# One 512 KB piece of V per batch is sent to the lower 64 partitions of two slots

## The chip, the core and the metric

The kernel runs on one core of a Trainium2 chip. The time is that of one execution on the device in microseconds (us). The core has five engines that take part here: PE (TensorE: matrix products and transposes into PSUM), DVE (VectorE), ACT (ScalarE), POOL (GpSimd), and SP (SyncE), which in this kernel issues every data transfer. Transfers are carried out by 16 DMA engines. A tile in SBUF has 128 partitions. Each transfer raises its semaphore by 16 when its data has landed.

## The reference

Two layers are applied one after the other to x of shape [8, 1, 448] (8 batches, one query position, 448 channels). Each layer is an attention block and an MLP block, with residual sums:

```
x = x + A(layernorm(x))      # attention against the caches
x = x + B(layernorm(x))      # small MLP with a shift mixer
x = x + A(layernorm(x))      # the same caches and weights again
x = x + B(layernorm(x))

A: q = (x @ wq) as 16 heads of 256; k, v: caches [8 batches, 8 kv heads, 4096 keys, 256], two query heads per kv head
   p = softmax(q k^T / 16);  o = p v;  result = o @ wo
```

All arrays are bf16. The caches are by far the largest: K and V of one kv head are 4096 x 256 values, 2 MB each, so each cache is 128 MB. Every key of a head counts alike, so the keys may be taken in any order, as long as K and V have the same one.

## The kernel before, in words

**Tiles.** A slab in SBUF is cut into 31 slots (`NSLOT`), each 128 partitions x 2048 bf16, that is 512 KB. A head's K or V (2 MB) is loaded as four pieces c = 0 to 3 of one slot each. Partition p of the four pieces holds the keys 32p to 32p+31, piece c the keys 8c to 8c+7 of these, so a piece is 128 rows of 4096 B in memory. `chunks` (L444) makes these pieces and says with `most` how many neighbouring pieces may go in one transfer (1, 2 or 4 slots in a row, with rows of 4, 8 or 16 KB).

**Stages.** The work is cut by layer, batch b (0 to 7), and pair m (0 to 3) of two kv heads s = 0, 1. For each of them `kpart` (L836) builds the transposes of K, the scores, the softmax; `vpart` (L1034) the product with V. In `kpart` most K pieces are transposed by DVE in 32 x 32 blocks (`square`, L911 to L914), a few by PE with an ACT copy (L889 to L893); the scores are matrix products with K as the fixed operand (L919 to L925). The probabilities are exponentiated into `pT` (L1006), transposed by PE and DVE (L1013, L1021). The few pieces whose K went through PE have their probabilities in other places, copied by POOL (L1010) or ACT (L1027); a buffer `pN` of its own (there are two, `NZ`) serves this in layer 0 for m = 2 and 3. `vpart` then takes four matrix products per piece of V (`pv`, L1081 to L1091): 8 columns of probabilities as the fixed operand, 512 columns of V as the moving one.

**Order.** Layer 0 of batch b, the small MLP between (`turn(b)`), layer 1 of batch b and layer 0 of batch b+1 are woven together by the lists at L1216 to L1245. K pieces of layer 0 for m = 1, 2, 3 stay in their slots for layer 1; K of m = 0 is loaded again there, and V is always loaded anew. K(1, b, 0) comes together with V(1, b, 1); V(1, b, 0) comes with the first K of batch b+1.

**Queues.** `Plan.schedule` (L168) is a planner that runs over all operations with a cost for each, gives every engine one fixed order, and gives every transfer its slot. A transfer waits on SP for the readers of its slot's former content, in the order of `order` (L1248), and the transfers behind it wait with it. All transfers go out on one queue that feeds all 16 DMA engines. On its engine an operation waits in order, by semaphores.

Of the kernel before, what the change touches and what calls it, by code (L numbers as in the profile page):

```python
# [3 lines left out]
P = 128  # L4
B = 8
# [6 lines left out]
NCH = 4  # L12
NSLOT = 31
SMALL = 218
SLOT = 2048
# [5 lines left out]
NN = ((1, 0, 1, 1), (0, 0, 1, 1))  # L21
NZ = 2
WIDE = ((1, 0),)
MOST = (4, 4, 4, 2)
DRY4 = 4000.0
STILL = (False, False)
# [46 lines left out]
class Unit:  # L73


    def __init__(self, name, emit, nbytes, slotted=True):
        self.name, self.emit, self.nbytes, self.slotted = name, emit, nbytes, slotted
        self.wide = None
        self.slot = self.sem = self.val = None
        self.op = None  # L80
        self.readers = []
        self.land = None
        self.evs = [None, None]
        self.raw, self.source = False, None
        self.group, self.lead, self.pair = [self], None, None


class Plan:
# [9 lines left out]
    def add(self, eng, emit, cost, reads=(), writes=(), banks=(), units=(), prio=None, name="", n=4):  # L98
        o = Op(eng, emit, cost, self.prio if prio is None else prio, self.turn, name)
        o.n = n  # L100
        for b in reads:
            for w in b.writers:
                o.deps[w] = True
            b.readers.append(o)
        for b in writes:
            for w in b.writers:
                o.deps.setdefault(w, w.eng == eng and eng != "pe")
            for r in b.readers:
                if r is not o:
                    o.deps.setdefault(r, False)  # L110
            if o in b.readers:
                b.readers = [o]
            else:
                b.readers = []
            b.writers = [o]
        for k in banks:
            if k.eng == eng:
                for d in k.before:
                    o.deps.setdefault(d, False)
                k.ops.append(o)  # L120
            else:
                for d in k.ops:
                    o.deps.setdefault(d, False)
                k.before, k.ops, k.eng = k.ops, [o], eng
        for u in units:
            if u.op is not None:
                o.deps[u.op] = True
            u.readers.append(o)
        o.deps.pop(o, None)
        self.ops.append(o)  # L130
        return o
# [227 lines left out]
def bass_interleave_layers__gqa_block_cached__mixer_s_mlp__decode_kernel(  # L359
# [25 lines left out]
    slab = sb("slots", [P, SLOT * NSLOT], bf)  # L385
    slots = [slab[:, SLOT * i:SLOT * i + SLOT] for i in range(NSLOT)]
# [6 lines left out]
    ident = sb("ident", [P, P], bf)  # L393
# [3 lines left out]
    pT = [sb(f"pT{i}", [P, 192], bf) for i in range(NP)]  # L397

    pN = [sb(f"pN{i}", [P, 48], bf) for i in range(NZ)]
# [17 lines left out]
    psS = [nc.alloc_psum_tensor(f"psS{i}", [P, 512], f32) for i in range(NS)]  # L417
    psV = [nc.alloc_psum_tensor(f"psV{i}", [P, 512], f32) for i in range(NV)]
# [3 lines left out]
    bS = [Bank() for _ in range(NS)]  # L422
    bV = [Bank() for _ in range(NV)]
    bT, bX = Bank(), Bank()

    plan = Plan()
    add = plan.add
# [13 lines left out]
    U_wo = [rows(f"wo{i}", wo_sb[:, 8 * i:8 * i + 8, :], wo_src[:, 8 * i:8 * i + 8, :], P * 7168 * 1.1) for i in range(4)]  # L441
    U_w4 = [rows("w4", w4_sb[:, :, :], B_w4.rearrange("(t m) n -> m t n", m=P), P * 12544 * 1.1)]

    def chunks(cache, b, h, name, skip=(), most=2):  # L444


        src = cache[b, h].rearrange("(p j) d -> p (j d)", p=P)

        def emit(e, u):
            c, n = int(u.name[-1]), len(u.group)  # L450
            return e.dma_start(slab[:, SLOT * u.slot:SLOT * (u.slot + n)], src[:, SLOT * c:SLOT * (c + n)])
        us = [None if c in skip else Unit(f"{name}{c}", emit, P * 4096) for c in range(NCH)]
        for i in range(0, NCH, most):
            group = [u for u in us[i:i + most] if u is not None]
            if len(group) == most:
                plan.load(group[0], mates=group[1:])
            else:
                for u in group:
                    plan.load(u)
        return us  # L460


    Bc = Buf()
# [41 lines left out]
    BpT, BpZ, Brc = ([Buf() for _ in range(NP)] for _ in range(3))  # L505
    BpN = [Buf() for _ in range(NZ)]
# [302 lines left out]
    free_p, free_n = list(range(NP)), list(range(NZ))  # L809
# [4 lines left out]
    def apart(t):  # L814

        return t.rearrange("p (a c u r) -> p a c r u", a=4, u=3, r=4)[:, :, :, :, 0:3:2]
# [19 lines left out]
    def kpart(at, layer, b, m, kept, most=2):  # L836
# [12 lines left out]
        nS[0] += 1  # L849
        p.x = x  # L850
        p.y = y = free_p.pop(0)
        p.z = z = free_n.pop(0) if layer == 0 and m > 1 else None
        plan.prio = at
        p.K, p.kload = [], []
        for s in range(2):
            us = chunks(A_k_cache, b, 2 * m + s, f"{n}K{s}", [c for c in range(NCH) if (s, c) in kept], most)
            for c in range(NCH):
                if (s, c) in kept:
                    p.K.append(kept[s, c])
                    continue  # L860
                u = us[c]
                if u.lead is None:
                    p.kload.append(u)
                if c >= nns[s]:
                    v = Unit(f"{n}J{s}{c}", None, 0)
                    v.source, u.raw = u, True
                    if c % 2 and c - 1 >= nns[s]:
                        v.pair, p.K[-1].pair = p.K[-1], v
                    p.K.append(v)
                else:  # L870
                    p.K.append(u)
# [153 lines left out]
        for c in range(nn if z is None else 0):  # L1025
            ss = slice(sum(c >= w for w in nns), 2)
            add("act", lambda e, c=c, ss=ss: e.activation(apart(pT[y])[:, :, c, :, ss], xs.rearrange("p (a c r s) -> p a c r s", a=4, c=4, r=4)[:, :, c, :, ss],  # L1027
                                                          ACT.Exp, scale=INV_SQRT_DH), 230, [], [BpT[y]], [bS[x]], prio=pr, name=n + f"pn{c}")
        add("pool", lambda g: g.partition_all_reduce(db, rs, P, ReduceOp.add), 450, [B_["pm"]], [B_["gm"]], prio=pr + 1, name=n + "db")
        R = add("dve", lambda e: e.reciprocal(rc, db), 70, [B_["gm"]], [Brc[y]], prio=pr + 1, name=n + "rc")  # L1030
        R.deps = {d: data or d.eng == "dve" for d, data in R.deps.items()}
# [2 lines left out]
    def vpart(at, p, still, bank, most, aside):  # L1034
# [2 lines left out]
        own_ = lambda s, c: z is not None and c < p.nns[s]  # L1037
        Bp = lambda s, c: [BpN[z]] if own_(s, c) else [BpT[y], BpZ[y]]
        plan.prio = at
        p.V = [u for s in range(2) for u in chunks(A_v_cache, b, 2 * m + s, f"{n}V{s}", (), most)]  # L1040
        p.vload = [u for u in p.V if u.lead is None]
        if layer == 0:
            out_, bo = o1[b % 2][:, 8 * m:8 * m + 8], Bo1[b % 2][m]
        else:
# [3 lines left out]
        if still:  # L1048
            x = bank
            for s in range(2):  # L1050
                for c in range(NCH):
                    u = p.V[NCH * s + c]

                    def pv(e, u=u, c=c, s=s):
                        for cc in range(2):
                            o = psV[x][:, 16 * s + 4 * c + 2 * cc:16 * s + 4 * c + 2 * cc + 2]
                            for j in range(8):
                                i = j * DH + cc * P
                                if c < p.nns[s]:
                                    w = apart(pN[z] if own_(s, c) else pT[y])[:, j // 2, c, 2 * (j % 2):2 * (j % 2) + 2, s]  # L1060
                                else:
                                    w = apart(pT[y])[:, j % 4, p.place(s, c), 2 * (j // 4):2 * (j // 4) + 2, s]
                                last = e.matmul(o, slots[u.slot][:, i:i + P], w, start=(j == 0), stop=(j == 7))  # L1063
                        return last
# [8 lines left out]
        else:  # L1073
# [3 lines left out]
            for s in range(2):  # L1077
                for c in range(NCH):
                    u = p.V[NCH * s + c]

                    def pv(e, u=u, c=c, s=s):  # L1081
                        for i in range(4):
                            o = 12 * (NCH * i + p.place(s, c)) + 4 * s
                            w = pN[z][:, 12 * i + 4 * s:12 * i + 4 * s + 8] if own_(s, c) else pT[y][:, o:o + 8]
                            if c < p.nns[s]:
                                v = slots[u.slot][:, 512 * i:512 * i + 512].rearrange("p (k d) -> p k d", k=2)
                            else:
                                v = slots[u.slot].rearrange("p (k j d) -> p j k d", k=2, j=4)[:, i]
                            last = e.matmul(psV[x][32 * i:32 * i + 8, :].rearrange("p (k d) -> p k d", k=2), w, v,  # L1089
                                            start=(s == 0 and c == 0), stop=(s == 1 and c == NCH - 1))  # L1090
                        return last  # L1091
                    o = add("pe", pv, 430, Bp(s, c), [], [bV[x]], [u], prio=at + 0.02 * (NCH * s + c), name=f"{n}V{s}{c}", n=4)
                    if s or c:
                        o.deps[first] = True
                    else:
                        first = o
# [24 lines left out]
                for d in Bq1[b].readers + Bq1[b].writers:  # L1121
                    O.deps.setdefault(d, False)
        free_p.append(y)
        if z is not None:
            free_n.append(z)

    Bst = [{k: Buf() for k in ("pm", "gm", "mx")} for _ in range(NS)]
    red, Bred = sf[:, 0:8], [Bs[k] for k in ("sq", "f", "f1")]
# [263 lines left out]
```

## Time and profile before

| what | value |
|---|---|
| median of 3 runs | 1098.31 us (1097.34 to 1099.51) |
| the profiled execution's own time | 1098.74 us |
| its span (first to last instruction) | 1095.7 us |
| DVE busy | 832.6 us, 76% of the span |
| PE busy (matrix products) | 756.3 us, 69% |
| ACT busy, POOL busy | 207.8 us, 71.4 us |
| data moved by DMA | 448.94 MB, mean 410 GB/s |
| time in packets of the data queue q1 | 98.4% of 16 engines over the span |

How to read it: shares are of the span. The busy time of the DMA engines is the time that their packets took, summed over the 16 engines, so 100% means that all 16 had a packet under way all the time. Queue q1 carries the data that SP's transfers ask for, q8 and q14 carry instructions of the program itself. The times of the profiled execution and of the runs differ by 0.43 us at the median; 0.2% of the time is 2.2 us.

### The profile page before, as it was taken

How to read it: one execution, taken by the hardware profiler on the slowest of the kernel's cores; microseconds unless marked ns; L12 is line 12 of the kernel's file. 1: busy time of each engine (PE TensorE's matmuls, PEld its weight loads, DVE VectorE, ACT ScalarE, POOL GpSimd, SP SyncE). 2: the span in 40 equal slices, each digit the busy share in tenths (PEclk: the TensorE clock that was granted, in tenths of full speed). 3: DMA queues.
4: the chain of work that ended last, by engine and by line, in shares of the span. 5: the costliest groups of instructions: out<-in, count | busy, mean ns of one | idle time of the engine just before them, and what ended most of it. 6: DMA issues, size and time to landing. Idle time of an engine off the chain costs nothing.

```text
span 1095.7 us, 33703 instructions
## 1 busy us (share of the span) xinstructions
PE 756.3 (69%) x15400; PEld 526.6 (48%) x15400; DVE 832.6 (76%) x1595; ACT 207.8 (19%) x314; POOL 71.4 (7%) x232
## 2 busy tenths in 40 slices
PE   2566586778577865867767787577666786676864
PEld 2355454465346543555436554355444654356533
DVE  4999459964997499955899469984799739995572
ACT  1032121112021211203112032121221121121210
POOL 0000000000000000000000000000100000000000
PEclk9997566556655665556655556555655566555665
DMA  9999999999999999999999999999999999999994
GB/s 353 406 419 420 395 406 426 422 412 408 429 423 415 412 425 427 421 405 409 424 426 420 411 412 429 426 417 394 427 427 423 419 399 428 427 422 411 410 427 176
DMA packets 54846, 448.94 MB, mean 410 GB/s; under 512 B 5536, under 2 KB 11568, under 8 KB 14128
## 3 DMA queue, kind: packets, MB, share of 16 engines
q1 hardware_dynamic: 54704, 446.80, 98.4%
q8 instruction: 120, 1.97, 0.7%
q14 instruction: 22, 0.18, 0.0%
HBM read 446.77 MB, written 0.01 MB: 408 GB/s over the span
## 4 chain that ended last, share of the span: by engine, by line
DVE 39%; DMA 24%; PE 21%; issue 9%; ACT 3%; POOL 0%; POOLq 0%; DVEq 0%
DVE slots L914 29%; DMA slots<-in_A_k_cache_dram 16%; DMA slots<-in_A_v_cache_dram 8%; PE psV L1089 6%; PE psS L923 5%; DVE pT L1021 2%; PE psT L678 2%; ACT slots L892 2%; PE psS L902 2%; DVE slots L1102 1%; PE psV L1063 1%; PE psT L607 1%; PE psK L832 1%; PE psT L1138 1%; DVE qe L643 1%
## 5 line engine op out<-in xcount | busy, mean ns | idle before, releaser
L914 DVE STREAM_TRANSPOSE slots<-slots 128x1024 bf16<-128x1024 bf16 x544 | 649.4, 1228 | 33.0 <-DMA slots<-in_A_k_cache_dram 24.3
L923 PE MATMUL psS<-qe,slots 128*128 128x8 bf16 x5760 | 225.3, 175 | 152.6 <-DVE slots L914 111.5
L923 PEld LDWEIGHTS psS<-qe,slots 128*128 128x128 bf16 x5760 | 191.1, 104 | 238.5 <-DVE slots L914 176.0
L1089 PE MATMUL psV<-slots,pT 128*8 128x512 bf16 x1528 | 181.1, 550 | 17.5 <-DMA slots<-in_A_v_cache_dram 9.5
L892 ACT COPY slots<-psK 128x1024 bf16<-128x1024 bf16 x80 | 78.8, 1014 | 168.0 <-PE psK L832 167.6
L832 PE MATMUL psK<-ident,slots 128*128 128x128 bf16 x640 | 74.2, 301 | 4.2 <-DMA slots<-in_A_k_cache_dram 4.1
L1100 ACT ACTIVATE slots<-psV 128x512 bf16<-128x512 f32 x48 | 29.0, 605 | 218.5 <-PE psV L1089 218.4
L985 POOL PARTITION_ALL_REDUCE small<-small x64 | 23.8, 372 | 693.5 <-DVE small L983 582.4
L832 PEld LDWEIGHTS psK<-ident,slots 128*128 128x128 bf16 x640 | 61.1, 138 | 7.0 <-DMA slots<-in_A_k_cache_dram 4.9
L1063 PE MATMUL psV<-pT,slots 128*128 128x2 bf16 x1568 | 50.9, 166 | 17.1 <-DMA slots<-in_A_v_cache_dram 15.9
L951 PE MATMUL psS<-slots,qe 128*8 128x512 bf16 x184 | 55.4, 587 | 6.7 <-DVE slots L914 5.4
L1063 PEld LDWEIGHTS psV<-pT,slots 128*128 128x128 bf16 x1568 | 47.3, 104 | 19.7 <-DMA slots<-in_A_v_cache_dram 16.1
L1089 PEld LDWEIGHTS psV<-slots,pT 128*8 128x8 bf16 x1528 | 31.5, 90 | 50.5 <-issue 20.9
L1021 DVE STREAM_TRANSPOSE pT<-psS 128x128 bf16<-128x128 bf16 x64 | 44.9, 702 | 6.5 <-PE psS L1013 4.7
L1006 ACT ACTIVATE pT<-psS 128x128 bf16<-128x128 f32 x56 | 15.5, 277 | 178.7 <-DVE psS L1003 178.6
L1066 DVE TENSOR_REDUCE small<-psV 128x8 f32<-128x32 f32 x16 | 2.8, 174 | 58.5 <-PE psV L1063 58.5
L1111 PE MATMUL psV<-same,slots 128*128 128x4 bf16 x320 | 14.0, 166 | 43.0 <-DVE slots L1102 36.9
L630 DVE TENSOR_TENSOR qe<-psT,small 128x32 bf16<-128x32 f32 x32 | 6.1, 190 | 48.2 <-PE psS L923 34.3
L902 PE MATMUL psS<-qo,slots 128*128 128x2 bf16 x768 | 27.8, 167 | 17.6 <-ACT slots L892 10.5
L1102 DVE TENSOR_TENSOR slots<-psV,slots 128x512 bf16<-128x512 f32 x48 | 32.3, 672 | 10.0 <-ACT slots L1100 10.0
L902 PEld LDWEIGHTS psS<-qo,slots 128*128 128x128 bf16 x768 | 24.0, 101 | 25.4 <-ACT slots L892 17.1
L1111 PEld LDWEIGHTS psV<-same,slots 128*128 128x128 bf16 x320 | 11.8, 102 | 49.2 <-issue 40.8
(170 smaller groups left out, 805.8 us busy)
## 6 DMA issues: line engine op xcount, KB each, us to landing
slots<-in_A_v_cache_dram SPq DMA_DIRECT2D x149, 1024.0 KB, 9.7
slots<-in_A_v_cache_dram SPq DMA_DIRECT2D x50, 2048.0 KB, 19.1
slots<-in_A_k_cache_dram SPq DMA_DIRECT2D x44, 2048.0 KB, 18.1
slots<-in_A_k_cache_dram SPq DMA_DIRECT2D x71, 1024.0 KB, 13.7
slots<-in_A_v_cache_dram SPq DMA_DIRECT2D x14, 512.0 KB, 8.1
wo_sb<-in_A_wo_dram SPq DMA_DIRECT2D x4, 896.0 KB, 19.5
wq_sb<-in_A_wq_dram SPq DMA_DIRECT2D x3, 1024.0 KB, 9.1
w_sb<-in_B_w_dram SPq DMA_DIRECT2D x1, 1568.0 KB, 16.9
```

The costliest lines, as they stand in the source:

```text
L832: last = e.transpose(tile[:, j * P:(j + 1) * P], slots[u.slot][:, o:o + P], ident[:, :])
L892: return e.copy(slots[u.slot][:, 1024 * t:1024 * t + 1024], tile)
L902: last = e.matmul(o, slots[u.slot][:, i:i + P], q, start=(cc == 0), stop=(cc == 1))
L914: return e.transpose(o, i)
L923: last = e.matmul(o, slots[u.slot][:, i:i + P], qe[:, 128 * k + 64 * s + 8 * g:128 * k + 64 * s + 8 * g + 8], start=(g == 0), stop=(g == 7))
L951: last = e.matmul(o, q, K[:, lo:hi + 1:hi - lo, :, g, :], start=(g == 0), stop=(g == 7))
L1021: add("dve", lambda e: e.transpose(pZ[:, :, 0:3:2].rearrange("p n s r -> p n r s"), psS[x][:, 128:192].bitcast(bf).rearrange("p (n r s) -> ...
L1063: last = e.matmul(o, slots[u.slot][:, i:i + P], w, start=(j == 0), stop=(j == 7))
L1089: last = e.matmul(psV[x][32 * i:32 * i + 8, :].rearrange("p (k d) -> p k d", k=2), w, v, start=(s == 0 and c == 0), stop=(s == 1 and c == ...
L1100: add("act", lambda e: e.activation(part(0), psV[x][:, :], ACT.Copy), 590, [], [Bhalf[0]], [bV[x]], [v], prio=at - 1, name=n + "ve0").targ ...
L1102: add("dve", lambda e: e.tensor_tensor(part(1), psV[x][:, :], part(0), ALU.subtract), 590, [Bhalf[0]], [Bhalf[1]], [bV[x]], [v], prio=at - ...
L1111: last = e.matmul(to[:, 4 * cc:4 * cc + 4].rearrange("p (s h) -> p s h", s=2), part(k // 2)[:, i:i + P], w, start=(k == 0), stop=(k == 3))
```

## The change

For one head (s = 0) of one pair (m = 0) per stretch of the program, namely in layer 0 for b = 0 and in layer 1 for b = 0 to 6, eight times in all (`LOW`):

- K and V of that head are read from memory in another order of the rows: the source's first dimension is now 16 (a) and its second 8 (i), with row 16 i + a of memory going to partition 8 a + i. K and V have the same order.
- Piece c = 3 of V is no longer one transfer to 128 partitions of one slot, but two transfers of 64 rows (256 KB each), each to partitions 0 to 63 of a slot of its own. Each one's source has 8 as its first dimension. So this piece takes two slots, and the pieces of this V go as one transfer of two slots, one of one slot, and the two halves.
- The probabilities for the second half (those of partitions 64 to 127) are brought down to partitions 0 to 63 by one matrix product with a part of the identity (`lo`), and copied by ACT into a `pN` buffer (`lc`).
- The product with that piece (`low`) is eight matrix products over 64 partitions in place of four over 128.

```diff
+LOWS, LOWC = 0, 3
+def LOW(layer, b, m, s):
+    return s == LOWS and m == 0 and (layer == 1 and b < B - 1 or layer == 0 and b == 0)
...
-    def chunks(cache, b, h, name, skip=(), most=2):
+    def chunks(cache, b, h, name, skip=(), most=2, low=False):
         src = cache[b, h].rearrange("(p j) d -> p (j d)", p=P)
+        if low:
+            src = cache[b, h].rearrange("(i a j) d -> a i (j d)", i=8, a=16)
...
+        if low and cache is A_v_cache:
+            def half(k):
+                return lambda e, u: e.dma_start(slots[u.slot][0:64, :], src[8 * k:8 * k + 8, :, SLOT * LOWC:SLOT * (LOWC + 1)])
+            most = 2
+            us[LOWC] = Unit(f"{name}{LOWC}", half(0), 64 * 4096)
+            us[LOWC].upper = Unit(f"{name}u{LOWC}", half(1), 64 * 4096)
...
+        if p.low:
+            low = psS[x][0:64, 192:208].rearrange("p (a r) -> p a r", a=4)
+            add("pe", lambda e: e.matmul(low, ident[:, 64:P], apart(pT[y])[:, :, p.place(LOWS, LOWC), :, LOWS], start=True, stop=True),
+                110, [BpT[y], Bc], [], [bS[x]], prio=pr, name=n + "lo", n=1)
+            add("act", lambda e: e.copy(apart(pN[zl])[0:64, :, 0, :, LOWS], low), 230, [], [BpN[zl]], [bS[x]], prio=pr, name=n + "lc")
...
+                    def low(e, u=u, c=c, s=s):
+                        for i in range(4):
+                            o, i_ = 12 * (NCH * i + p.place(s, c)) + 4 * s, 12 * i + 4 * s
+                            for w, v in ((pT[y][0:64, o:o + 8], u), (pN[p.zl][0:64, i_:i_ + 8], u.upper)):
+                                last = e.matmul(psV[x][32 * i:32 * i + 8, :].rearrange("p (k d) -> p k d", k=2), w,
+                                                slots[v.slot][0:64].rearrange("p (k j d) -> p j k d", k=2, j=4)[:, i], start=False, stop=False)
+                        return last
...
-                    o = add("pe", pv, 430, Bp(s, c), [], [bV[x]], [u], prio=at + 0.02 * (NCH * s + c), name=f"{n}V{s}{c}", n=4)
+                    if u.upper is not None:
+                        o = add("pe", low, 860, Bp(s, c) + [BpN[p.zl]], [], [bV[x]], [u, u.upper], prio=at + 0.02 * (NCH * s + c), name=f"{n}V{s}{c}", n=8)
+                    else:
+                        o = add("pe", pv, 430, Bp(s, c), [], [bV[x]], [u], prio=at + 0.02 * (NCH * s + c), name=f"{n}V{s}{c}", n=4)
```

More of the change, by code (lines that the diff above doesn't have):

```diff
@@ L85, in __init__ @@
         self.group, self.lead, self.pair = [self], None, None
+        self.upper = None
 class Plan:
@@ L442, in bass_interleave_layers__gqa_block_cached__mixer_s_mlp__decode_kernel @@
     U_w4 = [rows("w4", w4_sb[:, :, :], B_w4.rearrange("(t m) n -> m t n", m=P), P * 12544 * 1.1)]
-    def chunks(cache, b, h, name, skip=(), most=2):
+    def chunks(cache, b, h, name, skip=(), most=2, low=False):
         src = cache[b, h].rearrange("(p j) d -> p (j d)", p=P)
+        if low:
+            src = cache[b, h].rearrange("(i a j) d -> a i (j d)", i=8, a=16)
         def emit(e, u):
             c, n = int(u.name[-1]), len(u.group)
-            return e.dma_start(slab[:, SLOT * u.slot:SLOT * (u.slot + n)], src[:, SLOT * c:SLOT * (c + n)])
+            return e.dma_start(slab[:, SLOT * u.slot:SLOT * (u.slot + n)], src[..., SLOT * c:SLOT * (c + n)])
         us = [None if c in skip else Unit(f"{name}{c}", emit, P * 4096) for c in range(NCH)]
+        if low and cache is A_v_cache:
[4 more added lines that the diff above has]
+            us[LOWC].upper = Unit(f"{name}u{LOWC}", half(1), 64 * 4096)
         for i in range(0, NCH, most):
             group = [u for u in us[i:i + most] if u is not None]
-            if len(group) == most:
+            if len(group) == most and all(u.upper is None for u in group):
                 plan.load(group[0], mates=group[1:])
@@ L458, in chunks @@
                 for u in group:
-                    plan.load(u)
+                    for w in (u, u.upper):
+                        if w is not None:
+                            plan.load(w)
         return us
@@ L851, in kpart @@
         p.y = y = free_p.pop(0)
+        p.low = LOW(layer, b, m, LOWS)
         p.z = z = free_n.pop(0) if layer == 0 and m > 1 else None
+        p.zl = zl = free_n.pop(0) if p.low else None
         plan.prio = at
@@ L855, in kpart @@
         for s in range(2):
-            us = chunks(A_k_cache, b, 2 * m + s, f"{n}K{s}", [c for c in range(NCH) if (s, c) in kept], most)
+            us = chunks(A_k_cache, b, 2 * m + s, f"{n}K{s}", [c for c in range(NCH) if (s, c) in kept], most, LOW(layer, b, m, s))
             for c in range(NCH):
@@ L1039, in vpart @@
         plan.prio = at
-        p.V = [u for s in range(2) for u in chunks(A_v_cache, b, 2 * m + s, f"{n}V{s}", (), most)]
-        p.vload = [u for u in p.V if u.lead is None]
+        p.V = [u for s in range(2) for u in chunks(A_v_cache, b, 2 * m + s, f"{n}V{s}", (), most, LOW(layer, b, m, s))]
+        p.vload = [w for u in p.V if u.lead is None for w in (u, u.upper) if w is not None]
         if layer == 0:
@@ L1123, in vpart @@
         free_p.append(y)
-        if z is not None:
-            free_n.append(z)
+        for z_ in (z, p.zl):
+            if z_ is not None:
+                free_n.append(z_)
     Bst = [{k: Buf() for k in ("pm", "gm", "mx")} for _ in range(NS)]
```

## The prediction

> **What bounds the kernel now.** I read the page's DMA rows first, then short windows of the trace, then the chain that ended last and SP's waits.
>
> ```profile
> span 1095.7 us, 33703 instructions
> PE 756.3 (69%) x15400; PEld 526.6 (48%) x15400; DVE 832.6 (76%) x1595; ACT 207.8 (19%) x314; POOL 71.4 (7%) x232
> ...
> DMA  9999999999999999999999999999999999999994
> ...
> q1 hardware_dynamic: 54704, 446.80, 98.4%
> q8 instruction: 120, 1.97, 0.7%
> ```
>
> No compute engine is over 76%, while the data queue alone fills 98.4% of 16 engines. What is left of the span is the start and the last 14 us, after the last piece of V. So the time is bytes through DMA engines, and a late engine makes its transfer late.
>
> The records of the sixteen semaphore steps of each transfer tell the engines apart. One fetch of instructions (queue q8, 0.7% x 16 x 1095.7 / 120 = 1.02 us each) sets one engine back by about 1.5 us, and the fetches go round eight of the sixteen engines only. The spread of a transfer's sixteen landings therefore grows to 4.3 to 4.6 us ahead of a batch's small MLP, and falls back to about 2.1 us after it, when the queue is short and the eight early engines stand idle. The eight late ones never do: their landings follow at 2.48 us per 1 MB from start to end. Over the run, 120 x 1.5 / 8 = 22 us of fetching lies on each late engine, and the early ones idle about as long, 2.5 us per batch.
>
> ```profile
> 20.00:40.00 20.00, 7.53 (x175) 6.42 (x171) 17.96 (x30) 1.97 (x2) 0.82 (x2) 1.00 1.01 413
> 60.00:100.00 40.00, 28.65 (x558) 21.58 (x556) 39.29 (x53) 12.48 (x17) 2.70 (x9) 0.97 1.01 419
> ```
>
> ```profile
> 13.20:13.80 0.60, 0.60 (x9) 0.60 (x10) 0.53 (x4) 0.00 (x0) 0.00 (x0) 1.00 1.07 191
> 13.80:14.40 0.60, 0.60 (x9) 0.60 (x7) 0.53 (x4) 0.02 (x1) 0.00 (x0) 1.00 0.95 219
> 14.40:15.00 0.60, 0.60 (x8) 0.53 (x5) 0.11 (x1) 0.60 (x1) 0.00 (x0) 1.00 1.07 253
> ```
>
> The last two columns are the DMA engines' busy share and GB/s. The second fence is when the two tails of wq (L432, 256 KB each, each to 64 partitions) come in: the engines are as busy, and move half as much, 221 GB/s on the mean against 416. Their 4096 B packets take 288 ns on the mean; the same packets of 128-partition pieces take 163 ns. The two tails take 2.40 us from landing to landing, an ordinary 512 KB 1.25 us. So a full engine can be a slowed one: it depends on which partitions the 16 engines write at one moment.
>
> ```profile
> SPq L451 <- PE psV L1089: 284.6, 83, 11.8
> SPq L451 <- PE psS L923: 255.8, 79, 11.2
> ...
> SPq L1335 <- DVE slots L914: 42.4, 13, 4.5
> ```
>
> ```profile
> DMA to landing us min/median/max: 5.1/12.2/31.9
> ```
>
> SP waits mostly for slots, and a transfer (L451) is asked for a median 12.2 us before it lands: compute has that much cover outside the stretch around each small MLP.
>
> **The change, part by part.** The sum is made against the profiled execution, 1098.74 us (span 1095.7 and 3.0 around it), 0.4 us above the median.
>
> *Bytes from one half to the other.* If each half-transfer runs on eight engines, the same eight, these carry 64 KB of the piece each instead of 32 KB, 1.25 us more per batch (the landing step of 512 KB), and the other eight 1.25 us less. Eight times: 10 us each way. Where the eight are the early ones, the late ones lose 10 of their 22 us of lag, and both sets end about level: the path gets 10 us shorter, to 1088.7. Where they are the late ones, it gets 10 us longer, 1108.7. The trace doesn't name the engines. [...]
>
> *The new order of rows.* K (2 MB) and three pieces of V (1.5 MB) of the head now have 16 as their source's first dimension, the halves 8. [...] The trace of before has no such transfer. [...] Nothing says a gain below zero, since the ordinary packets already run at one steady pace (8 KB in 309 to 319 ns). I take a price near the tails', because these too depart from the ordinary deal, less what the engines are out of step: packets at 288/163 are 0.77 longer, and the early eight land within 0 to 0.9 us of each other, some 0.3 us of a 1.2 us phase, which takes off a quarter: 0.6. Cost per batch on the early eight: 3.5 MB x 1.25 us per 512 KB = 8.7 us, the halves 2.5 us, together 11.2 x 0.6 = 6.7 us; with the 1.25 us of bytes 7.95. Against it stand the 2.5 us per batch that they idle: 5.45 us net, eight times **43.6 us**. At 0.88 it is 8.6 x 8 = 69 us (1168); at 0.3, 17 us (1115); from 0.11 on (1.25 + 11.2 f = 2.5) it costs more than the idle time pays.
>
> [...] By the row of the ordinary transfers alone the sum would be 1088.7.
>
> *SP.* Each time one transfer of 2 MB becomes four, three issues more at 0.33 us, 1 us; SP waits for slots far longer. Nothing.
>
> *Slots.* One of 31 is lost while the halves are held. At a median 12.2 us ahead, one slot is 1.25 us of cover; it matters only around the small MLP, and these loads come after it. 0 to 1 us; taken as 0.
>
> *PE.* Eight products instead of four per piece: four more at 550 ns (L1089) is 2.2 us, and `lo` 0.28 us as L1013: 20 us in all of an engine with 340 us idle. It holds the slots of that V 2.2 us longer, under 12 us of cover; without the cover SP would issue 2.2 us later, 18 us in all.
>
> *ACT and pN.* `lc` is 0.28 us (as L1027), in order behind `lo`, which itself waits for DVE's L1021 (0.70 us); PE's next products stand behind it for at most that, 8 us in all beside DMA. Taking one of the two `pN` buffers makes POOL's L1010 wait for products that end a stage before it; POOL is 7% busy. Nothing on the path.
>
> *Fetches.* Some 80 more PE instructions, a third of one fetch. Nothing. The end after the last V (batch 7) is untouched.
>
> Sum: 1098.74 + 43.6 = 1142.3, against a median of 1098.31: **1142 us**.
>
> **The rivals.**
> *A, forecast, 0.57: the new deal collides.* For it: busy engines at half rate for the tails. Against it: the tails use 64 partitions on 16 engines; K here writes 128. 1142, own range 1112 to 1168.
> *B, 0.29: the loads run at full rate, and the bytes go to the early engines.* For it: all 128-partition loads so far run at full pace; the early eight idle 2.5 us per batch, what the shift takes up. The late eight get 1.25 us per batch back. It decides if the price stays under 0.11 of these loads. 1089, 1085 to 1096.
> *C, 0.08: full rate, but the eight are the late ones, or the halves are spread over all 16 engines as the tails are* (which costs 1.2 us per batch): 1098.7 + 10 = 1109.
> *D, 0.06: nothing measurable.* Late engines relieved, but the next slot reader is as late: around each small MLP the transfers are asked for about 4 us before their turn, so DMA could begin to wait for compute. 1097 to 1100.
>
> **How the numbers follow.** About 0.2% (2.2 us) is what a measurement of this kernel can tell from no change. Faster is B, 0.29. Same is D, 0.06. Slower is A and C, 0.65. The range leaves out what of B lies under 1087 (0.06) and of A above 1160 (0.1): 1087 to 1160.
>
> **What would show it.** For A: in the middle of each batch, while K and V of this head come in, the GB/s row falls well under 415 at a busy share of 1; q1 stays near 98% over a longer span; 4096 B packets take well over 163 ns; the spread of landings grows past 5 us, with the early set now the late one. For B: GB/s stays at 415 to 425 there, the spread ahead of the small MLP falls from 4.5 to about 2 us, and the GB/s dips after it get smaller. In both, the issues show 16 transfers of 256 KB from V, and a new line for the `low` products, 64 of them with 64 partitions. If the halves landed on both sets alike, C's second form holds. The prediction is wrong if the new order runs at the ordinary pace, or if half a rate there is made up because compute, not DMA, holds those stretches.

## The result, and the profile after

The changed kernel takes 1223.57 us (median of 6 runs, 1211.81 to 1238.33) against 1098.24 us (6 runs, 1097.34 to 1099.51): 1.111 times as long, 95% interval 1.105 to 1.117. The slowest run, 1238.33 us, is over 1.5% above the fastest and isn't in the ratio; the other five have a median of 1221.93 us. The forecast was 1142 us and the range 1087 to 1160, so direction and the slowed loads came out as rival A had them, and the size is nearly three times what was summed: +125.3 us instead of +43.6. The profiled execution took 1213.08 us (span 1211.3), 10 us under the median; terms that come from its trace are told against its own 115.6 us of extra span.

The GB/s row of the page of the kernel before, 40 slices of 27 us each:

```profile
GB/s 353 406 419 420 395 406 426 422 412 408 429 423 415 412 425 427 421 405 409 424 426 420 411 412 429 426 417 394 427 427 423 419 399 428 427 422 411 410 427 176
```

The page of the changed kernel: span, engines, DMA share and GB/s by slices of 30 us, the two queues, and the shares of the chain that ended last.

```profile
span 1211.3 us, 33788 instructions
...
PE 769.6 (64%) x15416; PEld 524.7 (43%) x15416; DVE 836.0 (69%) x1595; ACT 209.4 (17%) x322; POOL 71.4 (6%) x232
...
DMA  9999999999999999999999999999999999999994
GB/s 288 315 420 407 396 329 351 402 409 322 349 405 416 340 339 373 421 391 318 349 397 421 401 322 332 414 421 388 335 315 424 420 377 342 347 424 412 376 428 189
...
q1 hardware_dynamic: 57872, 446.80, 98.2%
q8 instruction: 121, 1.98, 0.7%
...
DMA 54%; DVE 18%; PE 15%; issue 7%; SPq 4%; ACT 2%; POOL 0%; POOLq 0%; DVEq 0%
```

The same bytes (446.80 MB), the same share (98.2% of a span that is 115.6 us longer), and eight dips, one per use of the new order, from about 415 to 290 to 350 GB/s. PE has 13 us more work and DVE 3; neither is what grew. In the chain that ended last DMA has 54% where it had 24%. Stretches of the changed kernel, columns: stretch, its length, busy time of PE, PEld, DVE, ACT and POOL (instructions), granted clock, DMA share, GB/s:

```profile
20.00:40.00 20.00, 10.20 (x278) 9.30 (x275) 15.86 (x25) 1.97 (x2) 0.39 (x1) 1.00 1.01 303
60.00:100.00 40.00, 23.71 (x374) 15.85 (x374) 32.58 (x41) 9.35 (x12) 2.15 (x7) 1.00 1.01 420
168.00:179.00 11.00, 6.26 (x195) 5.17 (x191) 3.46 (x6) 4.26 (x5) 0.38 (x1) 0.50 0.99 235
179.00:193.00 14.00, 8.30 (x207) 6.10 (x206) 12.14 (x23) 1.14 (x4) 1.89 (x6) 0.50 1.01 419
198.00:218.00 20.00, 10.22 (x130) 4.64 (x130) 17.61 (x25) 1.12 (x3) 0.92 (x3) 0.56 1.01 298
225.00:255.00 30.00, 21.43 (x434) 16.39 (x431) 28.23 (x40) 7.62 (x10) 2.13 (x7) 0.56 1.01 421
```

While K of a changed head comes in (third row) the engines are as busy as ever and move 235 GB/s; with V of that head (fifth row) 298; in between and after, the old 420. The first row, 303, answers to 413 in the first row shown of before. So in these places the time is lost at full busy share, and the GB/s row has no other dips of this kind. The granted clock of PE is no part of it: it is 0.50 both at 235 and at 419 GB/s.

SP's waits and the time from issue to landing of the slots' transfers show that compute doesn't hold DMA up:

```profile
SPq L460 <- PE psS L942: 310.3, 79, 20.0
SPq L460 <- PE psV L1122: 246.6, 63, 7.9
...
SPq L1372 <- DVE slots L933: 87.7, 15, 14.4
```

```profile
DMA to landing us min/median/max: 7.0/15.8/34.7
```

SP waits longer for slots (1045 us in all, where it was 963), but a transfer is asked for a median 15.8 us ahead of its landing, where it was 12.2: the queue is longer, not emptier.

The packets say where the time went. Taking the median packets of before (16 KB 613 ns, 8 KB 311, 4 KB 159) as the pace, what the packets took above it, per engine, was 2.5, 13.0 and 1.5 us by size before, and is 25.4, 85.3 and 15.9 us after. The growth is 109.6 us, nearly all of the 115.6. Of it 22.9 us lies on 16 KB packets, which belong to ordinary transfers alone.

### The profile page after: what moved, and what is told of

Same layout as the page of the kernel before. It is cut to its first block, busy times and chain, and to the rows that moved or that the text cites. A ratio compares the mean times of both kernels' runs of the same rounds, so it can differ in the third digit from the quotient of the medians.

```text
span 1211.3 us, 33788 instructions
## 1 busy us (share of the span) xinstructions
PE 769.6 (64%) x15416; PEld 524.7 (43%) x15416; DVE 836.0 (69%) x1595; ACT 209.4 (17%) x322; POOL 71.4 (6%) x232
## 3 DMA queue, kind: packets, MB, share of 16 engines
q1 hardware_dynamic: 57872, 446.80, 98.2%
## 4 chain that ended last, share of the span: by engine, by line
DMA 54%; DVE 18%; PE 15%; issue 7%; SPq 4%; ACT 2%; POOL 0%; POOLq 0%; DVEq 0%
DMA slots<-in_A_k_cache_dram 33%; DMA slots<-in_A_v_cache_dram 21%; DVE slots L933 12%; PE psV L1122 5%; SPq L437 3%; PE psS L942 3%; PE psT L695 1%; PE psV L1088 1%; PE psT L624 1%; DVE pT L1040 1%; ACT slots L911 1%; PE psS L921 1%; PE psK L849 1%; PE psT L1175 1%; DVE slots L1138 1%
## 5 line engine op out<-in xcount | busy, mean ns | idle before, releaser
L1122 PE MATMUL psV<-slots,pT 128*8 128x512 bf16 x1496 | 184.4, 558 | 42.0 <-DMA slots<-in_A_v_cache_dram 33.7
L1088 PE MATMUL psV<-pT,slots 128*128 128x2 bf16 x1568 | 50.6, 165 | 20.6 <-DMA slots<-in_A_v_cache_dram 19.8
L970 PE MATMUL psS<-slots,qe 128*8 128x512 bf16 x208 | 52.6, 599 | 4.4 <-DVE slots L933 4.4
L1175 PE MATMUL psT<-small,wo_sb 128*128 128x1 bf16 x1024 | 33.1, 166 | 2.7 <-DVE small L1151 1.5
```

The lines of the kernel that those rows point to most:

```text
L970: last = e.matmul(o, q, K[:, lo:hi + 1:hi - lo, :, g, :], start=(g == 0), stop=(g == 7))
L1175: last = e.matmul(psT[:, 4 * (2 * s + i) + c:4 * (2 * s + i) + c + 1], wo_sb[:, a, d0:d0 + P], o1[b % 2][:, a:a + 1], start=(k == 0), stop ...
```

## The experiments

The theory, rival A's mechanism (theory 1 in the expectations): engines that write neighbouring blocks of eight partitions get in each other's way (they collide), whatever memory they read from. How a source's dimensions deal its rows out is called the deal here; the traces don't name a packet's engine, so which partitions an engine writes is the author's reading of the dimensions, and no run shows it. What the runs measure is lost pace, and that is what "collide" stands for below. What stands against it: memory is what collides (rows 256 KB apart); the halves' eight engines or their partitions are to blame; bytes on late engines; slots, products and issues that were costed at nothing.

**p1: the forms by themselves.** No attention and no MLP is computed; x is copied to the output. Three transfers of one form at a time, then one MB in sixteen transfers of eight rows.

```diff
+ordr: cache[0, h].rearrange("(p j) d -> p (j d)", p=128)                 # 128 partitions
+low:  cache[1, i].rearrange("(i a j) d -> a i (j d)", i=8, a=16)         # as the change has it
+near: ...rearrange("(a t i) n -> a t i n", a=16, t=2)[:, 0]              # same partitions, rows adjacent in memory
+half: the order of low, first 8 of 16, to partitions 0 to 63
+tail: 64 ordinary rows to partitions 0 to 63
+step4, step8, step1: 16 transfers of 8 rows, to partitions 4, 8 and 1 apart
```

> No attention and no MLP are computed here: x is copied to the output, and SP loads parts of the K cache in eight forms, each into a tile of its own, waiting for one form before the next. Rows are of 8 KB; an ordinary one took 311 ns on an engine before. Forms ordr, low, near: 3 transfers of 1 MB each to 128 partitions; ordr with 128 as the source's first dimension, low in the changed kernel's order (16 x 8, an engine's eight rows 256 KB apart in memory), near with 16 x 8 too, but an engine's eight rows next to each other in memory. Theory 1 (where an engine's eight rows go to neighbouring partitions, engines collide in pairs): ordr 7.5 us and some 2 us of latency, low and near both about 15. Rival (the memory side is slow, rows far apart): low about 15, near 7.5. Forms half (8 x 8, 3 x 512 KB, to 64 partitions, eight engines) and tail (64 first, 3 x 512 KB to 64 partitions): without collisions half 7.5, tail 3.7; theory 1: half 15, tail 7.5. Forms step4, step8, step1: 1 MB by 16 transfers of 8 rows (eight engines, one row each) to partitions 4, 8 or 1 apart. [...]

The stretches of this probe in the order of the list (stretch, length, POOL, clock, DMA share, GB/s):

```profile
3.20:12.00 8.80, 0.00 (x0) 1.00 0.90 355
13.75:28.10 14.35, 0.00 (x0) 1.00 0.99 219
30.40:44.70 14.30, 0.00 (x0) 1.00 0.96 218
46.80:61.10 14.30, 0.00 (x0) 1.00 0.48 108
63.40:71.30 7.90, 0.00 (x0) 1.00 0.91 196
73.60:84.40 10.80, 0.00 (x0) 1.00 0.32 94
86.00:96.00 10.00, 0.00 (x0) 1.00 0.36 105
97.50:111.00 13.50, 0.00 (x0) 1.00 0.49 73
```

From first to last packet: 3 MB in the ordinary order 8.74 us, in the changed order 14.39, and 14.34 with the rows adjacent in memory. So it is the deal of the rows to partitions, not where they lie in memory: 1.88 us extra per MB when alone ((14.39 - 8.74) / 3; that 416/221, the tails' ratio of GB/s before, is 1.88 too is chance), 8 KB packets at a mean of 587 ns instead of 335. The halves (1.5 MB on eight engines, the DMA share 0.48) take 14.33, where as many bytes per engine in the ordinary order take 8.74; the tails' form on 16 engines takes 7.94 for 1.5 MB.

Of the last three forms the one to eight neighbouring partitions at a time was the slowest: its packets took 893 ns at the median (309 for the ordinary ones), where distances of 4 and of 8 gave 448 both. These two aren't a clean test, because SP needed as long to issue the sixteen as they took; the issues in SP's timeline (start, length, line, count):

```profile
72.11 10.70 SPq L45 DMA_DIRECT2D step<-in_A_k_cache_dram  x16
84.72 9.68 SPq L50 DMA_DIRECT2D step<-in_A_k_cache_dram  x16
96.51 5.44 SPq L54 DMA_DIRECT2D step<-in_A_k_cache_dram  x16
```

A transfer to partitions some way apart holds SP for 0.67 or 0.60 us, one to neighbours 0.34.

**e1: the order alone.** K and V of the eight heads in the new order, no halves; each V is two transfers of 1 MB, and nothing of `lo`, `lc` and `low` is there.

```diff
-        if low and cache is A_v_cache:
+            most = 2
+        if False:
...
-        p.low = LOW(layer, b, m, LOWS)
+        p.low = False
```

> The changed kernel with the new order of rows for K and V of the head, but the fourth piece of V as before in one slot (two transfers of 1 MB), and the products over 128 partitions. Theory 1: the order alone carries most of the loss, 4 MB per batch at about twice the time and neighbouring transfers dragged along, 1180 to 1220 us. Rival (the halves, their second slot and the added products are the cost): 1098 to 1110.

1200.92 us (1191.48 to 1203.02), ratio 1.0916, 95% 1.0869 to 1.0963. From e1's page:

```profile
span 1197.9 us, 33670 instructions
...
GB/s 297 317 423 417 393 324 334 420 402 326 339 394 409 359 343 328 427 410 355 349 393 423 405 333 347 427 420 403 335 351 426 419 394 358 340 425 412 386 428 200
```

The same dips, with no half anywhere: the order makes 102.9 of the 125.3 us (against the 1098.0 of before that was measured beside it). That is 12.9 us per batch on 4 MB that take 9.96 us ordinarily (4 x 2.49), a price factor of 1.29. Alone it would have been 4 x 1.88 = 7.5 us. The rest is looked for in p2.

**e2: the halves alone.** The ordinary order everywhere, the piece as two transfers of 64 rows; slots, `lo`, `lc` and the eight products as in the change.

```diff
-            src = cache[b, h].rearrange("(i a j) d -> a i (j d)", i=8, a=16)
+            pass
...
-                ... src[8 * k:8 * k + 8, :, SLOT * LOWC:SLOT * (LOWC + 1)])
+                ... src[64 * k:64 * k + 64, SLOT * LOWC:SLOT * (LOWC + 1)])
```

> The changed kernel with the ordinary order of rows (128 first) for K and for V, the fourth piece still as two transfers of 64 rows to the lower partitions of two slots, but with 64 as the source's first dimension, so that all 16 engines share them as they share the tails of wq; slots, lo, lc and the eight products as in the changed kernel. Theory 1: 512 KB at 2.4 instead of 1.25 us, eight times, with some drag on neighbours: +9 to +18 us, 1107 to 1117. Rival (halves are the main cost): over 1150.

1136.84 us (1130.04 to 1139.33), ratio 1.0329, 95% 1.0286 to 1.0371: 38.8 us for 4 MB in all, more than the theory's 1107 to 1117 and less than the rival's 1150. The growth of the 4 KB packets, the halves' own size, is 10.4 us per engine; 28 us lie on packets of 8 and 16 KB (7.4 and 20.6 us), which here are all in the ordinary order. This is where the theory first fell short: the neighbours of the slow transfers in the queue were slowed too.

**p2: neighbours.** Five transfers of 1 MB, the third in the changed order: once with all engines in step, once with a small pair ahead of them that was meant to set four engines back by 2.5 us (an estimate: 64 KB more for each, at the pace of 1 MB in 2.49 us). Also the change's pattern with four partitions per row group (32 as the source's first dimension) for comparison. Nothing else is computed.

```diff
+groups: "(i a j) d -> a i (j d)", i=4, a=32            # 3 MB
+quart:  six transfers of 32 partitions of that order    # 1.5 MB on eight engines
+base:   4 ordinary MB
+mixa:   2 ordinary, 1 changed (i=8, a=16), 2 ordinary
+four, mixb: 256 KB on four engines, then the same five
```

> No attention and no MLP are computed here: x is copied to the output, and SP loads parts of the K cache in five forms, one after the other. groups: 3 transfers of 1 MB with 32 x 4 rows; theory 1 says 7.5 us and about 2 of latency, the rival 15. quart: six transfers of 32 partitions, 256 KB each, eight engines; theory 1 says 7.5 us, colliding 15. base: four ordinary transfers of 1 MB, 10.0 us. mixa: two ordinary ones, one in the changed kernel's order, two ordinary ones, 1 MB each: without drag on the neighbours 10.0 + 4.8 = 14.8 us. four and mixb: the same five after two transfers that put four engines 2.5 us behind the others: without drag 17.3 us at most; if engines that are out of step drag ordinary transfers into the collision, 18.5 or more.

```profile
3.80:12.10 8.30, 0.00 (x0) 1.00 0.94 377
14.00:22.20 8.20, 0.00 (x0) 1.00 0.49 192
24.00:34.60 10.60, 0.00 (x0) 1.00 0.94 384
36.00:52.10 16.10, 0.00 (x0) 1.00 0.96 324
54.00:74.20 20.20, 0.00 (x0) 1.00 0.90 273
```

Blocks of four partitions over all 128 don't collide: 8.30 us for 3 MB, against 14.39 for blocks of eight. (The tails' form of p1, 64 rows to 64 partitions on 16 engines, does: 7.94 us for 1.5 MB.) Nor do eight engines by themselves (8.19 us at a share of 0.49, against 14.33). Base took 11.02 us from first to last packet, so five ordinary MB would take 11.02 + 2.49 = 13.5. With one changed MB among them it is 16.09: 2.6 us for it, where it cost 1.88 alone. With the small pair ahead, the landings are the safer measure: the first of the five already landed over 1 us late on all engines, and four of its sixteen landings only about 1.1 us behind the rest, not 2.5. From its last landing to that of the fifth there are 13.3 us, where four ordinary MB take 9.94, so 3.4 us go to the one changed MB; the same count in step gives 12.4 us, or 2.5. The price in units of its own 2.49 us is 0.76 alone, 1.00 to 1.04 among neighbours in step, 1.36 out of step, each from one execution. The 1.29 of e1 lies between the last two, and the kernel's engines are out of step: sixteen landings of a transfer lie a median 2.9 us apart before the change, 3.6 in e1, 4.2 after the change.

**e5: the order with blocks of four.** e1 with one size changed.

```diff
-            src = cache[b, h].rearrange("(i a j) d -> a i (j d)", i=8, a=16)
+            src = cache[b, h].rearrange("(i a j) d -> a i (j d)", i=4, a=32)
```

> The run with the order of rows alone, with one thing altered: 32 x 4 in place of 16 x 8, so that an engine can keep groups of four neighbouring partitions. Theory 1: 1097 to 1100 us, as the kernel before, where 16 x 8 took 1201. Rival (rows in another order than memory's are slow as such): about 1200 again.

1099.86 us (11 runs, 1098.19 to 1103.35), ratio 1.0013, 95% 1.0003 to 1.0023. From its page:

```profile
GB/s 346 407 419 420 398 400 425 421 390 406 425 424 414 404 426 426 423 406 408 426 428 419 416 411 426 426 419 396 425 427 425 419 395 427 427 421 412 412 426 178
```

The dips are gone. Against e1 only the length of the blocks of partitions differs, and with it go 101 us; the probes, with blocks of eight at 14.39 us (p1) and of four at 8.30 (p2), agree. What the engines meet at isn't shown by any run; that over all 128 partitions blocks of eight are slow, and of four not, is.

**e4: the whole change without the collision.** Blocks of four, so the piece goes as four transfers of 32 partitions (8 rows of the first dimension each, a form that ran at a share of 0.49 in p2); slots, `lo`, `lc`, `pN`, eight products and the lost transfer of 2 MB are as in the change.

```diff
-            src = cache[b, h].rearrange("(i a j) d -> a i (j d)", i=8, a=16)
+            src = cache[b, h].rearrange("(i a j) d -> a i (j d)", i=4, a=32)
...
+                    for g in range(2):
+                        last = e.dma_start(slots[u.slot][32 * g:32 * g + 32, :], src[16 * k + 8 * g:16 * k + 8 * g + 8, :, ...])
```

> The changed kernel with groups of four instead of eight neighbouring partitions: the rows of K and V of the head are taken with 32 as the source's first dimension and 4 as its second, and the fourth piece of V comes by four transfers of 32 partitions (8 x 4 rows each), two into the lower 64 partitions of each of the two slots. The bytes per engine, the slots, lo, lc and the eight products are the changed kernel's. Theory 1 (eight neighbouring partitions per engine make engines collide, four do not): the loss goes, and what the bytes are worth is left: 1088 to 1093 us if the eight engines are the early ones, 1105 to 1112 if they are the late ones. Rival (any order but the ordinary one, or any transfer on eight engines, is slow, or the added products and slots cost): over 1130.

1110.65 us (1110.27 to 1111.04), ratio 1.0111, 95% 1.0097 to 1.0125. That is 10.8 us over e5, where a shift of bytes to late engines was summed at 10. The landings show what the piece does: each pair of its transfers moves eight of the sixteen landings on by 1.26 us and leaves the other eight, and both pairs of a piece move the same eight. These eight aren't the late half: ahead of the piece of layer 1, b = 0, they are a mixed set, with the three earliest landings and the latest among them. Nor are they those that carry the instruction fetches: of some 18 landings that a fetch set back behind a piece, 11 were among those that the piece had not moved. But in 13 of 16 steps the last landing moved with them, and a transfer is complete only with its last landing. Over the eight pieces the last landing came 8 to 9 us later than pieces on 16 engines would have made it, and the sixteen lay 1.2 to 2.6 us further apart behind a piece than ahead of it. So 8 to 9 of the 10.8 us are the bytes. Slots, products, `lo`, `lc`, `pN` and four issues more per use are left with 1 to 3 us together, by subtraction. That such a transfer runs on eight engines shows elsewhere too: shares of 0.48 in p1 and 0.49 in p2, and p1's 616 packets under 512 B, which come out as eight for each of its 53 transfers of 8 or 8 x 8 rows and sixteen for each of the other 12.

**e3: eight rows at a time in the kernel before.** The piece goes to its usual slot by 16 transfers of 8 rows, partitions 4 apart; order, products and slots are as before.

```diff
+                for g in range(0, P, 32):
+                    for r in range(4):
+                        last = e.dma_start(slots[u.slot][g + r:g + 32:4, :], src[g + r:g + 32:4, SLOT * LOWC:SLOT * (LOWC + 1)])
```

> The kernel before, in which only the transfer of the fourth piece of V of the same eight heads is altered: 16 transfers of 8 rows each, to partitions 4 apart, into its usual slot and its usual partitions. Each runs on eight engines with one row each, so the same 32 KB per engine are moved from one half of the engines to the other as in the change, with no new order of rows and no new product; SP issues 13 to 15 transfers more per batch, some 5 us of its time. If the eight engines are the early ones (case B's mechanism without the collision): 10 us less, 1088 to 1093. If they are the late ones: 1105 to 1110. If SP's extra issues are felt: later by up to 5 us per batch, over 1120.

1126.34 us (1125.88 to 1126.87), ratio 1.0254, 95% 1.0237 to 1.0271. It was meant to show the shift of bytes alone, and doesn't: SP took some 10 us to issue the sixteen (0.67 us each), and across one piece (at 193 us) the earliest and the latest landing both moved on by 8.9 us, of which 4.9 are the next ordinary transfer and 1.27 the piece itself, so 2.7 us are lost there. Over the eight pieces the last landing lost 1.3 to 3.4 us at each, some 20 of the 28 us in all; the rest isn't placed. The slow issue and slowed packets (16 KB at 633 ns on the mean instead of 616) both have a part; the two weren't separated. For the shift of bytes e4 is the run to read.

**e6: the eight early engines.** e4, with the piece's four transfers (the quarters) going to the upper 64 partitions and issued by POOL, each behind a small one of 8 rows. The author took it that these would land on the other eight engines; no run shows it.

```diff
+                        e.dma_start(skip8[:, n_:n_ + 2], A_x[:, 0, n_:n_ + 2]).then_inc(sem8, 16)
+                        last = e.dma_start(slots[u.slot][64 + 32 * g:96 + 32 * g, :], src[16 * k + 8 * g:16 * k + 8 * g + 8, :, ...])
```

> The bytes moved the other way. [...] If the quarters land on the eight engines without instruction fetches, and the bytes are worth 10 us per 8 pieces as the quarters on the other eight cost 11: 1086 to 1092 us. [...]

1113.99 us (1113.48 to 1116.25), ratio 1.0145, 95% 1.0124 to 1.0167, so the hoped-for gain isn't there, and the run is 3.3 us over e4 too. That POOL, which works in order, held up the sums behind its transfers isn't excluded. From its page:

```profile
PE 756.9 (68%) x15416; PEld 521.7 (47%) x15416; DVE 834.4 (75%) x1595; ACT 209.7 (19%) x322; POOL 105.7 (10%) x296
...
q1 hardware_dynamic: 56720, 442.60, 97.3%
q0 software_dynamic: 3584, 4.20, 1.3%
```

The 4.20 MB did go by the other queue, and POOL is 34 us busier. The landings lie a median 2.8 us apart, against 2.7 in e5, so nothing shows that the quarters landed on the early engines, and whether balancing could gain anything stays open.

## Why the prediction was right or wrong

*What bounds it: right.* Bytes through DMA engines at a full share before and after; 98.4% and 98.2% of q1.

*The new order collides (A): right in kind, and the term that failed.* The signs that were read are there: GB/s well under 415 at a share of 1, 4 KB packets at a mean of 219 ns (170 before), the spread of a transfer's landings at up to 7.6 us. Whether the early engines became the late ones, which A said too, wasn't read. The price was taken as 0.6 of the loads' own time, with 0.88 (416/221 less 1) as the top. Both were the author's estimates from the tails, taken over to an order that no trace of before has, and no run shows either; e1 measured 1.29. The step that failed is the argument for its size: "engines are out of step", which was to take a quarter off. p2 shows the opposite sign: 1.04 in step, 1.36 out of step. And the top was no bound, because it priced only the changed transfers' own packets: 22.9 us of the growth lie on 16 KB packets of ordinary transfers. That engines out of step reach from one transfer into the next, and carry the collision there, fits this and the landings of p2, but is an argument that no run shows. With the own prices of p1 alone (3.5 MB x 1.88, the halves 14.33 / 8.74 on 2.5 us) A would have come to 6.6 + 1.6 us per batch; with the neighbours it was about 14.3 (below).

*The halves: same error.* After over e4 and e1: 125.3 less 90 (3.5 MB x 2.49 x 1.29 x 8) less 10.8 leaves 24.5, or 3.06 us per batch on 2.5, a factor of 1.23. This is a remainder, not a run of its own. In the ordinary order on 16 engines (e2) the halves alone cost 38.8.

*Bytes: the size near, the idle time wrong.* The forecast set 2.5 us per batch of idle time of the early eight against the price, that is 20 us in all, since it took the eight engines of a half for the early ones. That a half runs on eight engines, always the same, was a supposition then, and the runs bear it out: in the changed kernel's trace each of the 16 halves has eight landings, and in e4 both pairs of a piece moved the same eight landings by 1.26 us. That they are the early ones failed: without a collision the whole change should then have gained 10 us, and e4 lost 10.8. The eight that a half runs on are a mixed set, and the latest engine was among them in most steps, so there was no idle time to pay from. Rival C had the number, 1109, and e4 measured 1110.65; but its condition, that the eight are the late ones, isn't what the landings show, so the number was in part luck. From the forecast to the result:

```
forecast            8 x (11.2 x 0.60 + 1.25 - 2.5)               =  43.6
no idle time to pay from                                          + 20.0
price of 3.5 MB     8 x (8.7 x 1.29 - 8.7 x 0.6)                  + 48.0
price of halves     8 x (2.5 x 1.23 - 2.5 x 0.6)                  + 12.6
bytes and the rest  8 x (1.35 - 1.25)                             +  0.8
                                                                  = 125.0
```

*What was costed at nothing: right within 3 us.* Slots, `lo`, `lc`, `pN` and SP's issues come to 1 to 3 us together (e4 less e5, less the bytes). This is a remainder too. The new products and the copy are these groups (line, engine, operation, shapes, count, busy time, mean ns, idle before):

```profile
L1110 PE MATMUL psV<-slots,pN 64*8 64x512 bf16 x32 | 5.0, 598 | 0.0
L1110 PE MATMUL psV<-slots,pT 64*8 64x512 bf16 x32 | 4.6, 560 | 9.4 <-DMA slots<-in_A_v_cache_dram 9.4
...
L1053 ACT CAST pN<-psS 64x16 bf16<-64x16 f32 x8 | 1.3, 165 | 6.8 <-PE psS L1051 6.8
```

Sixty-four products of 64 partitions take what was said (550 ns each), and it is the data of V that they wait for, not the probabilities. One duration was off without harm: SP issues a transfer in the new order in about 0.6 us (p1: 1.92 us for three), not 0.33.

*The rivals.* B fell with e1 and e5: blocks of eight don't run at full pace (14.39 us against 8.74 in p1), and where the pace is full (e4) the bytes don't go to the early engines alone. D fell with the result.

*The range.* It ended at A's 0.88 bound less a chance. A range for a collision should have taken in what it does to the transfers around it, and the trace of before has the row for that. Around the two tails, from the last landing of the transfer of wq two ahead of them to the last landing of the K transfer behind them:

```profile
11.20:19.04 7.84, 4.38 (x107) 4.06 (x108) 2.79 (x24) 1.93 (x2) 0.00 (x0) 1.00 1.02 341
```

In these 7.84 us 2.5 MB land, which take 6.21 at 2.485 us per MB. That is 1.63 us more for 1.25 us of tails, a factor of 1.3, where the prediction read 0.77 to 0.88 from the tails' own packets and GB/s. The transfer of wq just ahead of them lands with its sixteen 1.46 us apart instead of 0.71. So the 1.29 of e1 could have been read before the run, from the tails with their neighbours.

## What to carry to other kernels

A full DMA share said nothing of the pace here (98.4% at 410 GB/s, 98.2% at 371): read GB/s and packet times beside it, place by place. The deal of a source's rows to partitions cost about a tenth of the run: 16 x 8 cost 103 us of 1098 where 32 x 4 cost 1. A transfer that collides must be priced with its neighbours in the queue, and here the more so where engines were out of step; the price from a probe by itself (0.76) was too low for the kernel (1.29).

## What the runs showed of the hardware that was not expected

The price of a collision went with how the engines stood to each other: 1.9 us alone, 2.6 among ordinary transfers, 3.4 with four engines about 1.1 us behind, for the same 1 MB. The times scatter with it: the changed kernel's runs without the highest span 1.4%, e1's 1.0%, those of the kernel before and of e4 0.2% and 0.1%. And a transfer whose first dimension is 8 had eight landings instead of sixteen (each of the changed kernel's 16 halves); the eight that e4's landings show are neither the early nor the late half, and as the latest landing was among them in 13 of 16 steps, such transfers added to a lag instead of filling a gap: 8 to 9 us here.
